# Cluster products with 32 moving columns, transform constants in six pieces, conversions at other steps, and a gated MLP without GpSimd's multiplication

## The chip, the core and the metric

The kernel runs on one core of a Trainium2 chip. The core has a matrix engine (PE, with PEld for its weight loads), three engines for elementwise work (DVE, ACT, POOL) and SP, whose queue issues most of the transfers (DMA); POOL issues a few as well. The metric is the time of one execution on the device, in microseconds (us), lower is better. Before the change it is 743.91 us (median of 3 runs, 739.0 to 745.26).

## What is computed

Three stages follow each other: attention in which a query sees only the keys of its own cluster, a Fourier mixing with a first MLP, and a second MLP with a convolution and a gate. All is float32; the matrix work is done with operands split into a high and a low part.

```python
# attention: B=2, H=8, S=768, D=64, 16 centroids per head
q_assign = argmax(einsum('bhsd,hcd->bhsc', q_n, c_n))   # and k_assign
mask   = q_assign[..., :, None] == k_assign[..., None, :]
scores = where(mask, scale * q @ k.T, -1e9)
attn   = softmax(scores) ; x = attn @ v                 # to [B, S, 512]
# mixing and first MLP (512 -> 2048 -> 512)
u  = x + real(fft(fft(x, axis=1), axis=2))
x  = u + relu(layernorm(u) @ w_ch1) @ w_ch2
# second MLP (512 -> 1024 -> 512)
h    = relu(x @ w_in)
gate = sigmoid(conv_w[0]*h[s-1] + conv_w[1]*h[s] + conv_w[2]*h[s+1])
out  = (h * gate) @ w_out
```

## The kernel before

**Attention in steps.** The 16 pairs of batch and head are cut into 6 tiles of 128 queries each, so there are 96 tiles, and one loop goes over steps n from -8 to 105. The order of all instructions in this part is the one written out by hand. In step n PE makes the scores of tile n+8 (`score_max`, L530 and L532) and DVE reduces them to the row maxima m (L535); PE makes the scores of tile n again, transposed (`score_exp`, L564 and L566), ACT takes their exponential (L572) and casts it to 16 bits (L584), POOL or, for tiles listed in `LO_ON_DVE`, DVE makes the low part (L592), and PE multiplies tile n-3 with the values (`attn_v`, L604). Three PSUM tiles of two banks take turns for all scores (`slot`), so PE can start a score only when the reduction or exponential of the third product back is done.

**Work that comes every 12 steps.** Two heads share one load, numbered m = 0 to 7. With k = 12m - 24, `load_raw` is issued at step k, `prep_sims` (the cluster products, L404, with a maximum L408 and a comparison L410 on DVE) at k+5, the high and low parts of q and k (`prep_hi`, `prep_lo`) at k+8 to k+11, `prep_turn` at k+11, `load_v` at k+14, `v_max` (a DVE reduction over the loaded values, L489) at k+16, and `v_turn` with four small DVE operations (`v_step`) at k+18. Four lists say where in a step something stands: `pre` before the scores, `mid` after PE's scores, `aft`, `post` and `fill` after the tile's own work. Every engine takes its instructions strictly in this order, so one that waits holds up all behind it.

**Cluster products.** `prep_sims` makes 12 products per pair of heads. Each loads 128 columns of q or k as weights and moves the centroid matrix W through, 128 columns of which only the first 32 are ever other than zero for this pair; a product's surplus columns are overwritten by the next.

**Conversions ahead.** The weights come as 64-bit words and are made into float32 by five operations (`from64`, L283 to L288; four on DVE and a square on ACT, L285). Four quarter loads of 512 columns are converted during attention: `ahead_start` issues the load three steps before the first operation, `ahead_store` writes the result to memory one step after the last. `AHEAD_STEPS` holds five steps for each of the four groups.

**Transform constants.** `DC` (two parts of 128 x 3342 float32) is loaded from POOL's queue at steps 20 and 32, `OD` at step 33; the first product that reads them is at step 60.

**Second MLP.** `mlp2_up` makes 128 of the 1024 hidden columns for 768 tokens: PE's product u, ACT's relu into h2 (L820), DVE's three convolution operations into cv (L822 to L824), ACT's sigmoid (L825), POOL's product with h2 (L826), and DVE's high and low part gH and gL (L828, L829). ACT casts the weights' high part (L792), POOL subtracts for the low part (L794). `down` multiplies gH and gL with w_out. PE's order is up 0, up 1, up 2, down 0, up 3, down 1 and so on, 16 of each over both batches; on the other engines the scheduler orders the work by its own rules.

Of the kernel before, what the change touches and what calls it, by code (L numbers as in the profile page):

```python
# [15 lines left out]
AF = mybir.ActivationFunctionType  # L16
ALU = mybir.AluOpType
# [2 lines left out]

B, H, S, D = 2, 8, 768, 64

DFT_LOADS = (20, 32)
LO_ON_DVE = {n for n in range(87) if n % 12 in (1, 2, 7, 11)} | {87}

AHEAD = 4
AHEAD_STEPS = [12 * q + n for q in range(4) for n in (17, 17, 18, 18, 22)]

IN_PLACE = range(89, 96, 2)
C = 16  # L30
# [9 lines left out]
C_CS, C_SS, C_CD, C_SD, C_END = 0, 1158, 2310, 2826, 3342  # L40
# [4 lines left out]
def tile_net(ctx, tc, qk, v, cen, w12, w34, conv, dft, odd, out):  # L45
    nc = tc.nc
    V, A, G, T = nc.vector, nc.scalar, nc.gpsimd, nc.tensor
# [264 lines left out]
    with ExitStack() as actx:  # L312
# [47 lines left out]
        t = slot("warm_up")  # L360
# [39 lines left out]
        def prep_sims(m):  # L400
            raw = raws[m]
            sm = sims[m] = first_bank("sim1") if m == 1 else slot(f"sim{m}")[:, 0]
            for t in range(12):
                T.matmul(sm[:, 32 * t:32 * t + 128], raw[:, t // 6, (t % 6) * 128:(t % 6) * 128 + 128],  # L404
                         W[:, m % 4, :], start=True, stop=True)
            sv = sm[:, 0:384].rearrange("p (g h c) -> p h g c", g=12, h=2)
            mx = ep.tile([128, 2, 12], F32, tag="mx", bufs=1, name=f"mx{m}")
            V.tensor_reduce(mx, sv, AX.X, ALU.max)  # L408
            eq = eqs[m] = ep.tile([128, 24, C], F16, tag="eq", bufs=1, name=f"eq{m}")
            V.tensor_tensor(eq.rearrange("p (h g) c -> p h g c", h=2), sv,  # L410
                            mx.unsqueeze(3).to_broadcast([128, 2, 12, C]), ALU.is_equal)
# [211 lines left out]
        def at(where, step, *f):  # L623
            where.setdefault(step, []).append(f)

        for m in range(1, NH // 2):
            k = 12 * m - 24
            if m > 1:
                at(pre, k, load_raw, m)
                at(post, k + 5, prep_sims, m)  # L630
                at(fill, k + 6, prep_first, m)
                at(fill, k + 7, prep_pick, m)
                at(fill, k + 8, prep_hi, m, (0,))
                at(fill, k + 9, prep_lo, m, 0, V)
                at(fill, k + 10, prep_hi, m, (1,))
                at(mid, k + 11, prep_turn, m)
                at(fill, k + 11, prep_lo, m, 1)
            at(fill, k + 14, load_v, m)
            at(fill, k + 16, v_max, m)
            at(mid, k + 18, v_turn, m)  # L640
            for i in range(4):
                at(aft, k + 18, v_step, m, i)
            at(fill, k + 22, v_step, m, 4)
            at(fill, k + 25, v_step, m, 5)
        at(fill, -8, prep_first, 1)
# [107 lines left out]
        for n in range(-LEAD, 6 * NH + 10):  # L753
# [11 lines left out]
            for f in aft.get(n, []) + post.get(n, []) + fill.get(n, []):  # L765
                f[0](*f[1:])
            if n in DFT_LOADS:
                i = DFT_LOADS.index(n)
                G.dma_start(out=DC[:, i], in_=dft[:, i])
            if n == DFT_LOADS[1] + 1:  # L770
                G.dma_start(out=OD, in_=odd)
            if n == 6 * NH - 10:
                ectx.close()
# [37 lines left out]
    def mlp2_up(b, f):  # L811
# [7 lines left out]
            up_half(o, w, xs[b], i)  # L819
            A.activation(h2[:, 1 + 384 * i:385 + 384 * i], o, AF.Relu)  # L820
        t = gp.tile([128, S], F32, tag="cv", bufs=2, name=f"cv{b}{f}")
        V.tensor_scalar(t, h2[:, 0:S], cw[:, 3 * f:3 * f + 1], None, ALU.mult)  # L822
        V.scalar_tensor_tensor(t, h2[:, 1:S + 1], cw[:, 3 * f + 1:3 * f + 2], t, ALU.mult, ALU.add)  # L823
        V.scalar_tensor_tensor(t, h2[:, 2:S + 2], cw[:, 3 * f + 2:3 * f + 3], t, ALU.mult, ALU.add)  # L824
        A.activation(t, t, AF.Sigmoid)  # L825
        G.tensor_mul(t, t, h2[:, 1:S + 1])  # L826
        g = hs[1, b, f] = [gp.tile([128, S], F32R, tag=n, bufs=2, name=f"{n}{b}{f}") for n in ("gH", "gL")]
        V.tensor_copy(g[0], t)  # L828
        V.tensor_sub(g[1], t, f32(g[0]))  # L829

    def down(s, g, f, side, when=(2,)):
# [163 lines left out]
```

## Time and profile before

| | |
|---|---|
| median of 3 runs | 743.91 us |
| profiled execution, its own time | 743.33 us |
| its span, first to last instruction | 741.5 us |
| PE busy | 694.9 us (94%) |
| DVE busy | 531.4 us (72%) |
| ACT busy | 346.8 us (47%) |
| POOL busy | 269.6 us (36%) |
| mean granted clock of PE | 0.984 of full |

Attention ends near 296 us, the first MLP near 589 us, the second at the end. A busy PE in this profile is one with a product in flight, not one at its peak. Idle times stand in square brackets behind an instruction, with what ended them.

### The profile page before, as it was taken

To read this page: it belongs to the slowest core of one execution; us is meant where nothing else is said; L and a number is where in the kernel's file an instruction comes from. 1 tells how busy PE (TensorE), PEld (TensorE's weight loads), DVE (VectorE), ACT (ScalarE), POOL (GpSimd) and SP (SyncE) were. 2 spreads that over 40 slices of the span, in tenths; PEclk is the share of its full clock that TensorE was granted. 3 is DMA by queue.
4 is the path that set the end of the run, shared out by engine and by line. 5 is a ranking of instruction groups with operands and counts; after the bars stand their busy time and mean duration, and the time that the engine had idled before them with its cause. 6 is when DMAs were issued, how large, how long until landed. Compare 5 with 4: busy or idle time off the path is not lost.

```text
span 741.5 us, 12519 instructions
## 1 busy us (share of the span) xinstructions
PE 694.9 (94%) x5090; PEld 618.4 (83%) x5090; DVE 531.4 (72%) x753; ACT 346.8 (47%) x493; POOL 269.6 (36%) x189
## 2 busy tenths in 40 slices
PE   8898999898898998989999999999999999999996
PEld 5697788787797886878988999999999888898984
DVE  7778989799977997999389938764111268777664
ACT  3476868586457687424234423443222233333321
POOL 8064544446244454121132012222332254444441
PEclk9999999999799999999999999999999999999999
DMA  7738678463532332324013421430000000002002
GB/s 213 183 71 213 183 198 248 121 179 79 151 78 58 89 107 95 114 77 179 29 44 127 156 72 61 166 114 1 1 0 1 1 0 1 1 1 85 1 1 85
DMA packets 19937, 66.47 MB, mean 90 GB/s; under 512 B 2868, under 2 KB 5928, under 8 KB 16808
## 3 DMA queue, kind: packets, MB, share of 16 engines
q1 hardware_dynamic: 19448, 61.93, 28.9%
q0 software_dynamic: 432, 3.75, 1.5%
q8 instruction: 40, 0.66, 0.4%
q14 instruction: 17, 0.14, 0.1%
HBM read 40.94 MB, written 5.77 MB: 63 GB/s over the span
## 4 chain that ended last, share of the span: by engine, by line
PE 45%; DVE 35%; DMA 5%; POOL 5%; ACT 4%; issue 3%; SPq 1%; POOLq 0%; DVEq 0%
DVE m L535 5%; PE acc L82 5%; DVE gH L828 5%; PE acc L80 5%; PE acc L81 5%; PE up L82 5%; PE up L80 5%; PE up L81 5%; DMA vraw<-v 4%; POOL cv L826 3%; PE av L604 3%; DVE cv L823 2%; DVE cv L824 2%; PE t L564 2%; PE s L530 2%
## 5 line engine op out<-in xcount | busy, mean ns | idle before, releaser
L592 POOL TENSOR_TENSOR p<-p,p 128x768 f16<-128x768 f32 x61 | 108.3, 1778 | 113.2 <-ACT p L584 83.0
L572 ACT ACTIVATE p<-t,cbias 128x768 f32<-128x768 f32 x92 | 82.7, 899 | 51.7 <-PE t L566 50.9
L535 DVE TENSOR_REDUCE m<-s 128x1 f32<-128x768 f32 x96 | 90.1, 943 | 11.7 <-PE s L532 6.6
L80 PE MATMUL up<-un,wha 128*128 128x384 f32 x248 | 84.2, 340 | 1.5 <-DVE firste L809 0.7
L82 PE MATMUL up<-un,wla 128*128 128x384 f32 x248 | 83.9, 339 | 1.6 <-DVE wla L794 1.6
L794 POOL TENSOR_TENSOR wla<-wa,wha 128x1024 fp32r<-128x1024 f32 x16 | 38.5, 2407 | 126.5 <-ACT wha L792 126.5
L81 PE MATMUL up<-un,wha 128*128 128x384 f32 x248 | 83.8, 338 | 0.0
L809 DVE SCALAR_TENSOR_TENSOR hL<-up,hH 128x384 fp32r<-128x384 f32 x62 | 34.2, 551 | 65.5 <-ACT hH L808 65.4
L604 PEld LDWEIGHTS <-p 128*128 128x128 f16 x1728 | 60.1, 99 | 18.0 <-issue 15.5
L584 ACT CAST p<-p 128x768 f16<-128x768 f32 x88 | 73.0, 830 | 1.4
L604 PE MATMUL av<-V,p 128*128 128x65 f16 x1728 | 71.7, 196 | 2.0 <-POOL p L592 2.0
L80 PE MATMUL acc<-wha,hH 128*128 128x512 f32 x186 | 73.6, 396 | 0.0
L82 PE MATMUL acc<-wha,hL 128*128 128x512 f32 x186 | 72.6, 391 | 0.0
L81 PE MATMUL acc<-wla,hH 128*128 128x512 f32 x186 | 72.5, 390 | 0.0
L564 PE MATMUL t<-X 128*128 128x384 f32 x192 | 55.6, 371 | 15.5 <-DVE m L535 14.1
L808 ACT ACTIVATE hH<-up 128x384 fp32r<-128x384 f32 x62 | 30.5, 491 | 75.7 <-PE up L82 75.6
L530 PE MATMUL s<-X 128*128 128x384 f32 x192 | 56.8, 377 | 5.9 <-DVE m L535 4.9
L828 DVE CAST gH<-cv 128x768 fp32r<-128x768 f32 x16 | 35.4, 2212 | 31.3 <-POOL cv L826 31.3
L792 ACT CAST wha<-wa 128x1024 fp32r<-128x1024 f32 x31 | 32.6, 1050 | 52.2 <-PE acc L82 46.2
L826 POOL TENSOR_TENSOR cv<-cv,h 128x768 f32<-128x768 f32 x16 | 25.5, 1591 | 78.0 <-ACT cv L825 78.0
L564 PEld LDWEIGHTS t<-X 128*128 128x128 f32 x192 | 31.8, 193 | 24.2 <-DVE m L535 15.2
L566 PE MATMUL t<-Y 98*128 98x384 f32 x192 | 50.9, 347 | 0.1
(314 smaller groups left out, 1644.3 us busy)
## 6 DMA issues: line engine op xcount, KB each, us to landing
rawa<-w SPq DMA_DIRECT2D x14, 1024.0 KB
rawb<-w SPq DMA_DIRECT2D x8, 1024.0 KB
raw<-qk SPq DMA_DIRECT2D x7, 768.0 KB
X<-G SPq DMA_DIRECT2D x14, 384.0 KB
Y<-G SPq DMA_DIRECT2D x14, 384.0 KB
DC<-dft POOLq DMA_DIRECT2D x2, 1671.0 KB, 7.0
vraw<-v SPq DMA_DIRECT2D x8, 384.0 KB
out<-y SPq DMA_DIRECT2D x12, 256.0 KB
```

The source lines that it names most:

```text
L80: T.matmul(o, sH, mH, start=start, stop=False)
L81: T.matmul(o, sH, mL, start=False, stop=False)
L82: T.matmul(o, sL, mH, start=False, stop=stop)
L530: T.matmul(t[:, c, 0:384], X[:, 0, sl], X[:, 1, 384 * c:384 * c + 384], start=True, stop=False)
L535: V.tensor_reduce(m6s[h][:, i:i + 1], t[:, :, 0:384], AX.XY, ALU.max, negate=True)
L564: T.matmul(t[:, c, 0:384], X[:, 1, sl], X[:, 0, 384 * c:384 * c + 384], start=True, stop=False)
L566: T.matmul(t[:, c, 0:384], Y[0:98, 1, sl], Y[0:98, 0, 384 * c:384 * c + 384], start=False, stop=True)
L572: A.activation(p, t[:, :, 0:384], AF.Exp, bias=cbias, scale=0.125)
L584: A.copy(p16[:, 0], p32s[n])
L592: eng.tensor_sub(p16[:, 1], p, p16[:, 0])
L604: T.matmul(o, p16[:, k, 128 * j:128 * j + 128], v16[:, i, h % 2, 65 * part:65 * part + 65], start=(i + j + k + part == 0), stop=(i == 5), ...
L828: V.tensor_copy(g[0], t)
```

## The change

The cluster products move 32 columns of W instead of 128. The constants DC are loaded in six pieces at steps 8, 20, 21, 32, 33 and 44, and OD at step 45. The first group of conversions stands at steps 10, 10, 11, 11, 13, and the other three where groups one to three stood before, so each group is a period of 12 steps earlier or nearly so and none is left in steps 53 to 58. `v_max` goes from k+16 to k+17, `v_turn` and the first four `v_step` from k+18 to k+19. In the second MLP the first convolution operation goes from DVE to ACT, the gate's product from POOL to DVE, and the cast to gH from DVE to ACT.

```diff
-DFT_LOADS = (20, 32)
+DFT_LOADS = (8, 20, 21, 32, 33, 44)
-AHEAD_STEPS = [12 * q + n for q in range(4) for n in (17, 17, 18, 18, 22)]
+AHEAD_STEPS = [10, 10, 11, 11, 13] + [12 * q + n for q in range(1, 4) for n in (5, 5, 6, 6, 10)]
...
             for t in range(12):
-                T.matmul(sm[:, 32 * t:32 * t + 128], raw[:, t // 6, (t % 6) * 128:(t % 6) * 128 + 128],
-                         W[:, m % 4, :], start=True, stop=True)
+                T.matmul(sm[:, 32 * t:32 * t + 32], raw[:, t // 6, (t % 6) * 128:(t % 6) * 128 + 128],
+                         W[:, m % 4, 0:32], start=True, stop=True)
...
-            at(fill, k + 16, v_max, m)
-            at(mid, k + 18, v_turn, m)
+            at(fill, k + 17, v_max, m)
+            at(mid, k + 19, v_turn, m)
             for i in range(4):
-                at(aft, k + 18, v_step, m, i)
+                at(aft, k + 19, v_step, m, i)
...
             if n in DFT_LOADS:
-                i = DFT_LOADS.index(n)
-                G.dma_start(out=DC[:, i], in_=dft[:, i])
-            if n == DFT_LOADS[1] + 1:
+                i, part = divmod(DFT_LOADS.index(n), 3)
+                part = slice(*((C_CS, C_SS), (C_SS, C_CD), (C_CD, C_END))[part])
+                G.dma_start(out=DC[:, i, part], in_=dft[:, i, part])
+            if n == DFT_LOADS[-1] + 1:
                 G.dma_start(out=OD, in_=odd)
...
-        V.tensor_scalar(t, h2[:, 0:S], cw[:, 3 * f:3 * f + 1], None, ALU.mult)
+        A.activation(t, h2[:, 0:S], AF.Copy, scale=cw[:, 3 * f:3 * f + 1])
...
-        G.tensor_mul(t, t, h2[:, 1:S + 1])
+        V.tensor_mul(t, t, h2[:, 1:S + 1])
...
-        V.tensor_copy(g[0], t)
+        A.copy(g[0], t)
```

On DVE around step 28 (m is the row maxima of two neighbouring tiles, vsc the maximum over the loaded values, U the attention's output, mx and eq the work on the cluster products), before:

```order
L535 TENSOR_REDUCE m_6_1427<-s_1428 128x1
L489 TENSOR_REDUCE vsc_1468<-vraw_1387 128x1
L617 SCALAR_TENSOR_TENSOR U<-av_1165,vsc_473,d_1389 128x6x64
L535 TENSOR_REDUCE m_6_1427<-s_1471 128x1
L283 TENSOR_SCALAR ahead<-ahead 128x512
L284 SCALAR_TENSOR_TENSOR ahead<-ahead 128x512
L408 TENSOR_REDUCE mx_1520<-sim_1507 128x24
L410 TENSOR_TENSOR eq_1522<-sim_1507,mx_1520 128x384
L535 TENSOR_REDUCE m_6_1427<-s_1529 128x1
```

The same place after the change:

```order
L535 TENSOR_REDUCE m_6_1436<-s_1437 128x1
L617 SCALAR_TENSOR_TENSOR U<-av_1173,vsc_525,d_1398 128x6x64
L535 TENSOR_REDUCE m_6_1436<-s_1478 128x1
L283 TENSOR_SCALAR ahead<-ahead 128x512
L284 SCALAR_TENSOR_TENSOR ahead<-ahead 128x512
L408 TENSOR_REDUCE mx_1527<-sim_1514 128x24
L410 TENSOR_TENSOR eq_1529<-sim_1514,mx_1527 128x384
L489 TENSOR_REDUCE vsc_1531<-vraw_1396 128x1
L535 TENSOR_REDUCE m_6_1436<-s_1538 128x1
```

The reduction over the values (L489) has moved behind one row maximum, two conversions and the work on the cluster products.

On DVE around step 11, in the first period of 12 steps (G is the low part of k in `prep_lo`), before:

```order
L535 TENSOR_REDUCE m_3_688<-s_689 128x1
L617 SCALAR_TENSOR_TENSOR U<-av_413,vsc_175,d_649 128x6x64
L535 TENSOR_REDUCE m_3_688<-s_732 128x1
L461 TENSOR_TENSOR G_647<-raw_337,G_647 128x768
L535 TENSOR_REDUCE m_3_688<-s_783 128x1
```

The same place after the change:

```order
L535 TENSOR_REDUCE m_3_691<-s_692 128x1
L283 TENSOR_SCALAR ahead<-ahead 128x512
L284 SCALAR_TENSOR_TENSOR ahead<-ahead 128x512
L617 SCALAR_TENSOR_TENSOR U<-av_413,vsc_175,d_651 128x6x64
L535 TENSOR_REDUCE m_3_691<-s_737 128x1
L286 SCALAR_TENSOR_TENSOR ahead<-ahead 128x512
L461 TENSOR_TENSOR G_649<-raw_337,G_649 128x768
L535 TENSOR_REDUCE m_3_691<-s_790 128x1
```

Three conversion operations have come in, one of them (L286, behind ACT's square) directly ahead of `prep_lo`.

On ACT in the second MLP, one hidden block in the second batch (h is the relu, cv the convolution and sigmoid, whb the weights' high part), before:

```order
L820 ACTIVATE h_7438<-u_7441 128x384
L820 ACTIVATE h_7438<-u_7455 128x384
L825 ACTIVATE cv_7469<-cv_7469 128x768
L792 CAST whb_5_7560<-wb_6212 128x1024
L820 ACTIVATE h_7501<-u_7504 128x384
```

The same block after the change:

```order
L821 ACTIVATE h_7442<-u_7445 128x384
L821 ACTIVATE h_7442<-u_7459 128x384
L823 ACTIVATE cv_7473<-h_7442,cw 128x768
L826 ACTIVATE cv_7473<-cv_7473 128x768
L793 CAST whb_5_7564<-wb_6216 128x1024
L829 CAST gH_7479<-cv_7473 128x768
L821 ACTIVATE h_7505<-u_7508 128x384
```

ACT has two more operations in a block, the first convolution operation ahead of the sigmoid and the cast to gH behind the weight cast; on PE only the width of the cluster products and the step of `v_turn` differ, beside two products of the first `down` that change places.

## Rows read from the trace of the kernel before

**Rows 1.** Page, part 1: busy us (share of the span) xinstructions, first engines.
```profile
PE 694.9 (94%) x5090; PEld 618.4 (83%) x5090; DVE 531.4 (72%) x753; ACT 346.8 (47%) x493; POOL 269.6 (36%) x189
```
**Rows 2.** Waits of the whole run: who waited for whom, us, times, longest.
```profile
DVE vsc L489 <- DMA vraw<-v: 13.0, 4, 4.8
```
**Rows 3.** Timeline 127 to 143 us: start, us, engine, what, [idle before].
```profile
132.45 2.92 PE L404 MATMUL sim<-W,raw 128*128 128x128 f32 x24
...
135.57 0.95 DVE L489 TENSOR_REDUCE vsc<-vraw 128x1 f32<-128x768 f32 x1 [4.83 <-DMA vraw<-v]
...
137.96 1.01 PE L530 MATMUL s<-X 128*128 128x384 f32 x2 [2.59 <-DVE m L535]
```
**Rows 4.** Stretches: us, busy PE, PEld, DVE, ACT, POOL, granted clock, DMA share, GB/s.
```profile
138.00:141.00 3.00, 3.00 (x10) 2.81 (x10) 2.89 (x6) 0.00 (x0) 0.89 (x1) 0.50 0.42 88
186.00:196.00 10.00, 8.04 (x53) 6.95 (x54) 9.92 (x12) 3.56 (x5) 3.52 (x3) 0.50 0.43 114
```
**Rows 5.** Tile "ahead", its DVE operations: ns min/median/max, first and last start us.
```profile
L283 DVE TENSOR_SCALAR ahead<-ahead x4: 415/417/417, 73.1 to 170.3; 128x512 int32<-128x512 int32 x4
L284 DVE SCALAR_TENSOR_TENSOR ahead<-ahead x4: 692/693/694, 73.5 to 170.7; 128x512 int32<-128x512 int32 x4
...
L286 DVE SCALAR_TENSOR_TENSOR ahead<-ahead x4: 672/673/2105, 76.8 to 174.0; 128x512 uint32<-128x512 uint32 x4
L288 DVE SCALAR_TENSOR_TENSOR ahead<-ahead x4: 682/842/1005, 84.4 to 189.9; 128x512 f32<-128x512 f32 x4
```
**Rows 6.** Timeline of PE, 176 to 190 us: two products that had waited.
```profile
177.06 0.62 PE L564 MATMUL t<-X 128*128 128x384 f32 x2 [1.09 <-DVE m L535]
...
186.82 0.98 PE L564 MATMUL t<-X 128*128 128x384 f32 x2 [2.99 <-DVE m L535]
```
**Rows 7.** Timeline 54 to 61 us, DVE and PE in steps 11 and 12.
```profile
55.60 0.96 DVE L535 TENSOR_REDUCE m<-s 128x1 f32<-128x768 f32 x1 [1.95 <-ACT ohT L431]
56.47 2.41 DVE L461 TENSOR_TENSOR G<-raw,G 128x768 fp32r<-128x768 f32 x1
...
59.80 0.62 PE L564 MATMUL t<-X 128*128 128x384 f32 x2 [0.86 <-DVE m L535]
```
**Rows 8.** Timeline of PEld, 43 to 46 us: weight loads of 16-bit and 32-bit tiles.
```profile
43.70 0.61 PEld L604 LDWEIGHTS <-p 128*128 128x128 f16 x18 [0.16 <-issue]
44.25 0.30 PEld L530 LDWEIGHTS s<-X 128*128 128x128 f32 x2
```
**Rows 9.** Instructions by line and form: cluster products' loads, and constants' issues on POOL.
```profile
L404 PEld LDWEIGHTS sim<-W,raw 128*128 128x128 f32 x168 | 19.3, 192 | 0.6 <-ACT W L383 0.6
L769 POOL DMA_DIRECT2D DC<-dft x2 | 1.3, 673 | 0.0
```
**Rows 10.** Waits of PE, 580 to 742 us: us, times, longest.
```profile
PE acc L80 <- DVE gH L828: 1.6, 1, 1.6
PE acc L82 <- DVE gL L829: 1.4, 2, 1.1
PE acc L80 <- DVE y L847: 1.1, 1, 1.1
PE u L80 <- DVE x L868: 1.0, 1, 1.0
```
**Rows 11.** One DVE round of the second MLP as a stretch, columns as in Rows 4.
```profile
699.80:708.87 9.07, 9.07 (x47) 8.11 (x46) 6.32 (x7) 2.56 (x4) 3.94 (x2) 1.00 0.00 0
```
**Rows 12.** Timeline of PE: the first product of two neighbouring up blocks.
```profile
700.38 0.34 PE L80 MATMUL u<-x,whb 128*128 128x384 f32 x1
...
708.82 0.34 PE L80 MATMUL u<-x,whb 128*128 128x384 f32 x1
```
**Rows 13.** By line and form: count, busy us, mean ns, idle before; elementwise work of one tile.
```profile
L824 DVE SCALAR_TENSOR_TENSOR cv<-h,cw,cv 128x768 f32<-128x768 f32 x16 | 16.3, 1017 | 0.5
L829 DVE TENSOR_TENSOR gL<-cv,gH 128x768 fp32r<-128x768 f32 x16 | 15.3, 957 | 1.3
L510 ACT ACTIVATE V<-vraw,vsc 128x768 f16<-128x768 f32 x8 | 7.4, 922 | 0.7 <-DVE vsc L508 0.7
```

## The prediction

> **What bounds the kernel now.** I read the page's busy times first. PE has a product in flight for 694.9 of 741.5 us [rows 1], so little can be won that is not PE's own time or a stretch in which PE stands still. By stage, the timeline shows two kinds of loss in attention, which is the first 296 us. One is a DVE that waits: four of the eight reductions over the loaded values (L489) stand still for their transfer, 13.0 us in all, the longest 4.8 us [rows 2], and DVE takes its work in order, so the row maxima behind them are late. The other is a DVE with too much to do in one place, around 177 to 192 us. In both cases PE runs out of free score tiles: it has three, and the third product back must have been reduced. What PE then loses it loses twice, since its granted clock falls to half of 2.4 GHz: 0.50 in 138 to 141 us and through 186 to 196 us [rows 4], each after a standstill of 2.6 to 3 us [rows 3, 6]. In the second MLP PE comes to a new up block every 8.44 us [rows 12], while one DVE round takes 9.07 us [rows 11]; PE is ahead by two blocks, so it stands still only at the start, where the batches change, and at the end [rows 10].
>
> **v_max one step later.** Take the longest wait. The reduction stands from 130.7 to 135.6 us, and the products for the clusters run on PE from 132.45 to 135.4 [rows 3]. Then PE stands for 2.59 us, because the next row maximum (0.95 us) and what follows it are behind the reduction. After the change DVE first makes that row maximum, two conversions (0.42 and 0.69 us [rows 5]) and the cluster work, and comes to the reduction only behind PE's last cluster product at 135.4 us, when the values have landed or nearly so. The scores are then released before PE is done with the cluster products. The row maximum behind the reduction comes one reduction (0.95 us) later than it could, most of it beside PE's next scores; I leave 0.3 us for it, so 2.3 of 2.59 us go. With no such standstill the clock should not fall: the 3 us at half speed [rows 4] hold 1.5 us of work at full speed. Term: **-3.8 us**. Below it is nothing, if the conversions now ahead of the reduction wait for their own load, which is queued just in front of the values; above it is -6, if the smaller standstills behind the other three waits go as well. I take the case counted out here. The four small operations of v_step and the turn go a step later and have until step k+22; that slack is the cover, and without it the values would be scaled one step late, 2.7 us a load if 296 us are spread over some 110 steps.
>
> **Conversions.** No group is left in steps 53 to 58. There the last group took 0.42, 0.69, 2.10 and 0.68 us of DVE [rows 5] (of L286 the longest, which is its last, and of L288 the shortest, as it began at 189.9), 3.9 us together, 3.2 of them before PE's long wait at 186.8. PE stood for 1.09 and 2.99 us there [rows 6], and DVE was busy for 9.92 of the 10 us from 186 to 196 [rows 4], so its work sets the pace and what is taken from it comes back. Of 3.9 us I count 3.3, because DVE then meets PE's own pace sooner. Below is nothing. Above is -9: both standstills (4.1 us) and half of the ten slow microseconds (5). I stay near the lower end because the mixing's folds in the same steps keep DVE full.
>
> The first group now stands in steps 10 to 13. Its first two operations, 1.1 us, fall into the 1.95 us in which DVE waits for ACT [rows 7], so they cost nothing; without that wait they would cost their 1.1. The third needs ACT's square of the same step and stands ahead of prep_lo. By the rows, prep_lo began at 56.47 and the next row maximum only after its 2.41 us, and PE had already stood 0.86 us [rows 7]. The third operation adds its 0.67 us [rows 5] and about 1.2 us of waiting for the square, less what prep_lo regains if POOL is no longer at work beside it. Term: **+1.5 us**, between +0.5 and +4 (2.4 us of waiting and work, and a fallen clock at 1.5). The store of this group now stands ahead of the next load and of the values on SP's queue and waits for the conversion in step 13. Behind it are the load of the second group and the values of m = 2; these have the step that v_max was given, about 2.5 us, as cover, and if it is gone the first wait of rows 2 stays as it was. Conversions: **-1.8 us** together.
>
> **Cluster products with 32 columns.** Each float32 product is two instructions, 24 for a pair of heads: 168 loads for seven pairs [rows 9], 2.92 us to the end of the last [rows 3], so one comes every 0.115 us. With a quarter of the columns the moving part would shrink, but every instruction also loads 128 columns of 32-bit weights. The trace shows how fast such loads can follow each other where nothing holds them: two of them take 0.30 us [rows 8], one alone takes 0.19 [rows 9], so the second starts 0.11 us after the first. The weight load then sets the pace: 24 x 0.11 = 2.64 instead of 2.76 us, and the last product ends some 0.08 us sooner. That is 0.2 us a pair, eight pairs: **-1.5 us**, and nothing where DVE is behind anyway. The other bound is the 16-bit tiles, where 18 loads take 0.61 us [rows 8], 0.03 us each: 24 x 0.033 = 0.8, or 2 us less a pair, 16 in all. I stay with the nearest row, since it is the same form of load.
>
> **Constants in six pieces.** The bytes are the same. Four more issues at 0.67 us of POOL [rows 9] make 2.7 us on an engine that is idle for most of the span [rows 1], so I count nothing; where POOL had a low part waiting, each would delay it by 0.67. All pieces are issued by step 45, fifteen steps ahead of their first use.
>
> **Gated MLP.** PE's standstills for gH and gL are 1.6 and 1.4 us, of which 1.9 stand at the end, where DVE's slower rounds have used up PE's lead; those for x and y are 1.0 and 1.1 [rows 10]. The new round: ACT's work in one DVE round is 2.56 us [rows 11], and it gains the first convolution operation (0.92 us, by a scaled pass of the same size) and the cast to gH (0.83 to 0.92), so some 4.3 us. Between them DVE has two multiply-adds of 1.02 us; its new product of 0.96 us lies beside the weight cast on ACT [rows 13]. That makes 6.4 us with a little for the hand-overs, less than PE's 8.44, so PE's lead holds to the end. Of 3.0 us for gH and gL I count 2.7, of x all of 1.0, of y half: **-4.2 us**. If a DVE operation with two inputs is drawn out by POOL's subtraction as prep_lo was (2.41 us [rows 7] against 0.96 [rows 13]), the round grows to 7.9 us and still fits. Bounds: -2 (two such stretches, 9.3 us, and the end as now) and -5.1, all four waits.
>
> **The sum.** -3.8 - 1.8 - 1.5 - 4.2 = -11.3 us against 743.3 us of the profiled execution (span 741.5 and 1.8 around it), which is 0.6 us under the median: **732.0 us**.
>
> **Rivals.**
> *The loads do not bind (faster).* If 32 columns bring the products to the pace of the 16-bit tiles, 14.4 us more go, less what DVE holds back in its full stretches: 717.6 at the best and about 720. For it speaks that loads and products overlap well; against it the 0.30 us of rows 8. The Trainium skill, page "TensorE: Matmul & The Clock Gate", section "Back-to-back issue gap", gives a start-to-start floor of about 25 ns for 1 to 64 columns; by it a pair would take 0.6 us. [...]
> *The clock falls (slower).* A cluster product now moves a quarter of the columns in about the same 2.6 us. If the granted clock drops behind each of the seven products in the loop, and stays down for 10 us as at 186 us [rows 4], each costs 5 us: 732 + 35 = 767. If it stays down for 3 us as at 138, each costs 1.5: 742.5, no change. It decides from 2.8 us a product (19.3 us to the bound of slower, over seven). Against it: there was no standstill in these places, and PE's other work stands close on both sides.
> *The waits come back.* The conversions now ahead of v_max wait for their load, SP is held by the store, and the last steps of attention's heavy period stay full for the folds: the first two terms become +1.5 in place of -5.6 and the rest stays: 739. For it speaks that this load is queued just in front of the values.
>
> **Chances.** My forecast 0.56 (its own range 725 to 737), the loads that do not bind 0.13, the fallen clock 0.15 (0.07 of it slower, 0.08 no change), the waits that come back 0.16. About 1%, 7.4 us, is what a measurement of this kernel can tell from no change. Faster: 0.56 less 0.02 at its edge, 0.13, and 0.05 of the last: 0.72. No change: 0.02, 0.08 and 0.11: 0.21. Slower: 0.07. The range that holds 8 in 10 reaches from 718, inside the first rival, to 741, inside the last two.
>
> **What would show it.** Right: waits of L489 for vraw under 3 us in all; no half clock at 138 and less than 5 us of it near 186; PE's standstill in step 12 up to 2 or 3 us; cluster products at 2.6 to 2.8 us; no wait for gH or gL at the end, and DVE rounds of 8.4 us in the second MLP. Wrong: cluster products near 1 us, a granted clock of 0.50 behind them, conversions that wait for their load in step 17, or ACT as what PE waits for in the second MLP.

## The result and the profile after

The changed kernel takes 734.35 us (median of 4 runs, 733.92 to 736.4) beside 743.42 for the kernel before: a ratio of 0.9895, with a 95% interval of 0.986 to 0.993 (the quotient of the two medians is 0.988; the range below goes by the ratios). Six more runs of it later gave 734.59 us and 0.9875 (0.984 to 0.991). So it is faster, by 7.8 to 9.3 us where 11.3 were forecast: 734.35 against 732.0, inside the range. Two terms of the sum were wrong by more than that 2.4 us, in opposite directions.

The page of the changed kernel, part 1, which answers to [rows 1]:

```profile
PE 696.4 (95%) x5090; PEld 623.2 (85%) x5090; DVE 526.9 (72%) x737; ACT 376.2 (51%) x525; POOL 245.2 (33%) x177
```

PE is busy for 1.5 us longer although the span is 9.3 us shorter (732.2 against 741.5), and although its cluster products move only a quarter of the columns. Products that move less and take longer point to a lower clock.

To see where time is won and lost, I compare the start of the same instruction in both traces. The exponentials of ACT (one for each tile) serve in attention; later it is PE's first up product and its last product.

| place in the program | before, us | after, us | difference | change since the row above |
|---|---|---|---|---|
| exponential of tile 0 | 29.50 | 31.49 | +1.99 | +1.99 |
| tile 6 | 43.96 | 45.73 | +1.77 | -0.22 |
| tile 15 | 65.00 | 69.49 | +4.49 | +2.72 |
| tile 39 | 127.85 | 132.12 | +4.27 | -0.22 |
| tile 42 | 141.42 | 141.34 | -0.08 | -4.35 |
| tile 51 | 162.44 | 163.31 | +0.87 | +0.95 |
| tile 60 | 193.78 | 192.07 | -1.71 | -2.58 |
| first up product, second MLP | 589.01 | 587.33 | -1.68 | +0.03 |
| end of PE's last product | 736.70 | 727.37 | -9.33 | -7.65 |

Attention, forecast at -7.1 us, gives 1.7. The second MLP, forecast at -4.2, gives 7.65. Four rows of the table carry the story.

**Ahead of the loop: +2.0 us, with the clock at half.** Stretches of the changed kernel (us, busy PE, PEld, DVE, ACT, POOL, granted clock, DMA share, GB/s): the one ahead of the loop, one behind the cluster products of the pair m = 3, and the two of [rows 4]:

```profile
9.40:19.60 10.20, 10.20 (x50) 9.01 (x50) 5.43 (x13) 2.82 (x5) 6.72 (x6) 0.50 0.68 153
77.60:81.00 3.40, 3.40 (x27) 3.09 (x26) 3.37 (x6) 2.00 (x3) 0.91 (x1) 0.50 0.99 192
137.00:141.00 4.00, 4.00 (x34) 3.92 (x32) 3.97 (x3) 1.26 (x2) 2.84 (x2) 1.00 0.88 182
186.00:196.00 10.00, 8.25 (x63) 7.27 (x62) 8.93 (x11) 4.12 (x6) 2.74 (x3) 0.66 0.59 132
```

Before the change, the stretch from 9.40 to 19.60 ran at 1.00, and the second set of cluster products in it took 2.94 us:

```profile
9.40:19.60 10.20, 9.00 (x65) 7.59 (x66) 7.86 (x16) 3.83 (x6) 6.72 (x6) 1.00 0.80 184
```

```profile
9.72 2.94 PE L404 MATMUL sim<-W,early 128*128 128x128 f32 x24 [0.42 <-DMA early<-qk]
```

The timeline of PE in the changed kernel at the start of the first two stretches (start, us, engine, what):

```profile
9.17 5.00 PE L404 MATMUL sim<-W,early 128*128 128x32 f32 x24
14.10 1.45 PE L441 MATMUL fm<-ident,oh 128*16 128x128 f16 x12
...
73.48 0.73 PE L604 MATMUL av<-V,p 128*128 128x65 f16 x18
74.05 2.84 PE L404 MATMUL sim<-W,raw 128*128 128x32 f32 x24
76.73 0.60 PE L530 MATMUL s<-X 128*128 128x384 f32 x2
77.16 0.52 PE L532 MATMUL s<-Y 96*128 96x384 f32 x2
77.52 0.74 PE L564 MATMUL t<-X 128*128 128x384 f32 x2
78.06 0.84 PE L566 MATMUL t<-Y 98*128 98x384 f32 x2
```

None of these rows has an idle time in brackets. From 9.4 us on the clock is at half, right after the second set of cluster products has begun at 9.17, and the set takes 5.00 us; at 77.6 it falls 0.7 us behind such a set. PE had not stood still just ahead of either place. The falls of [rows 4] came with standstills of 2.6 to 3 us.

The 1.99 us of the table are not the price of this fall alone. The start of the first exponential lies anywhere from 27.60 to 30.99 us in the eleven traces, of the kernel before and of the experiments below, that have 64 or 128 columns here and the full clock. A closer measure is from the start of the second set to the first scores (L530): 8.11 us in the changed kernel against 5.98 before, so the fall costs 2.1 us up to there. (It is 7.6 in the two other traces with 32 columns here, and 5.8 to 6.0 in nine of the eleven. In the other two, e4 and e10, it is 7.3 and 7.1, since PE there waits 1.6 and 1.4 us for DVE.)

**Behind the long wait: -4.35 us.** L489 no longer waits for vraw anywhere, and at 138 the clock is full. The changed kernel's timeline there:

```profile
136.54 1.65 POOL L592 TENSOR_TENSOR p<-p,p 128x768 f16<-128x768 f32 x1
136.71 1.77 DVE L283 TENSOR_SCALAR ahead<-ahead 128x512 int32<-128x512 int32 x1
136.90 2.84 PE L404 MATMUL sim<-W,raw 128*128 128x32 f32 x24
138.37 1.65 POOL L592 TENSOR_TENSOR p<-p,p 128x768 f16<-128x768 f32 x1 [0.18 <-ACT p L584]
138.51 2.06 DVE L284 SCALAR_TENSOR_TENSOR ahead<-ahead 128x512 int32<-128x512 int32 x1
139.58 0.59 PE L530 MATMUL s<-X 128*128 128x384 f32 x2
140.49 0.55 DVE L408 TENSOR_REDUCE mx<-sim 128x24 f32<-128x384 f32 x1
141.54 0.94 DVE L489 TENSOR_REDUCE vsc<-vraw 128x1 f32<-128x768 f32 x1
```

PE goes from its cluster products straight into scores (no bracket at 139.58, where [rows 3] had 2.59 us). But the two conversions that now lie in DVE's former wait take 1.77 and 2.06 us, not 0.42 and 0.69 [rows 5]. Experiment e12 below shows why: POOL's subtractions (L592) run beside them.

**Steps 10 to 15: +2.7 us,** of which 0.8 belong to `v_max` (e4 below). DVE, POOL and PE of the changed kernel where the first group of conversions now stands, to be read against [rows 7]:

```profile
56.02 2.03 DVE L284 SCALAR_TENSOR_TENSOR ahead<-ahead 128x512 int32<-128x512 int32 x1
...
58.93 1.66 POOL L592 TENSOR_TENSOR p<-p,p 128x768 f16<-128x768 f32 x1 [1.43 <-ACT p L584]
...
59.37 1.77 DVE L286 SCALAR_TENSOR_TENSOR ahead<-ahead 128x512 uint32<-128x512 uint32 x1
61.06 0.95 DVE L461 TENSOR_TENSOR G<-raw,G 128x768 fp32r<-128x768 f32 x1
...
62.93 0.61 PE L564 MATMUL t<-X 128*128 128x384 f32 x2 [1.09 <-DVE m L535]
```

The third conversion no longer waits for ACT's square, as I had counted, since L284 ahead of it takes 2.03 us; it is itself drawn out by 1.1 us. PE stands at 59.50, 62.93 and 66.04, 2.8 us in all.

**Second MLP: -7.65 us.** What PE waits for in the changed kernel from 580 us to the end is one row, and [rows 10] are gone:

```profile
PE u L82 <- POOL wlb L795: 1.6, 1, 1.6
```

This row stands at the head of the stage in both kernels. One DVE round of the changed kernel as a stretch, against 9.07 us in [rows 11], and then, from its timeline, POOL's subtraction in that round with the gate's low part beside it:

```profile
690.98:699.42 8.44, 8.44 (x44) 7.62 (x43) 5.43 (x6) 4.55 (x6) 2.43 (x1) 1.00 0.00 0
```

```profile
694.95 2.43 POOL L795 TENSOR_TENSOR wlb<-wb,whb 128x1024 fp32r<-128x1024 f32 x1 [6.00 <-ACT whb L793]
...
695.83 2.37 DVE L830 TENSOR_TENSOR gL<-cv,gH 128x768 fp32r<-128x768 f32 x1 [0.77 <-ACT gH L829]
```

The stretch is as long as PE's own pace, 8.44 us, even with gL drawn out from 0.96 [rows 13] to 2.37 us.

### The profile page after: what moved, and what is told of

It is laid out like the page before. It is cut to its first block, busy times and chain, and to the rows that moved or that the text cites. A ratio compares the mean times of both kernels' runs of the same rounds, so it can differ in the third digit from the quotient of the medians.

```text
span 732.2 us, 12502 instructions
## 1 busy us (share of the span) xinstructions
PE 696.4 (95%) x5090; PEld 623.2 (85%) x5090; DVE 526.9 (72%) x737; ACT 376.2 (51%) x525; POOL 245.2 (33%) x177
## 4 chain that ended last, share of the span: by engine, by line
PE 65%; DVE 26%; issue 3%; POOL 2%; ACT 2%; DMA 1%; SPq 0%; DVEq 0%; POOLq 0%; ACTq 0%
PE acc L80 8%; PE acc L81 8%; PE acc L82 8%; DVE m L535 6%; PE up L82 5%; PE up L80 5%; PE up L81 5%; PE av L604 3%; PE u L82 3%; PE u L80 3%; PE u L81 3%; PE sim L404 2%; PE s L530 2%; PE t L564 2%; PE s L532 2%
## 5 line engine op out<-in xcount | busy, mean ns | idle before, releaser
L592 POOL TENSOR_TENSOR p<-p,p 128x768 f16<-128x768 f32 x61 | 106.5, 1748 | 117.9 <-ACT p L584 79.6
L795 POOL TENSOR_TENSOR wlb<-wb,whb 128x1024 fp32r<-128x1024 f32 x16 | 39.0, 2446 | 96.4 <-ACT whb L793 79.4
L530 PE MATMUL s<-X 128*128 128x384 f32 x192 | 58.5, 387 | 1.1 <-DVE m L535 0.8
L532 PE MATMUL s<-Y 96*128 96x384 f32 x192 | 51.2, 349 | 0.0
```

The costliest lines, as they stand in the source:

```text
L530: T.matmul(t[:, c, 0:384], X[:, 0, sl], X[:, 1, 384 * c:384 * c + 384], start=True, stop=False)
L532: T.matmul(t[:, c, 0:384], Y[0:96, 0, sl], Y[0:96, 1, 384 * c:384 * c + 384], start=False, stop=True)
L592: eng.tensor_sub(p16[:, 1], p, p16[:, 0])
L795: eng.tensor_sub(wl, w32[k, f], f32(wh))
```

## Experiments

All ratios are to the kernel before, measured on the same chip, with 95% intervals.

### e1 and e2: only the width of the cluster products

e1 is the changed kernel with wide products, e2 the kernel before with narrow ones.

```diff
-                T.matmul(sm[:, 32 * t:32 * t + 32], raw[...], W[:, m % 4, 0:32], ...)   # e1
+                T.matmul(sm[:, 32 * t:32 * t + 128], raw[...], W[:, m % 4, :], ...)
```

> The changed kernel with only the cluster products put back to 128 moving columns. Theory A (the narrow products let the granted clock fall: in the changed kernel it stands at 0.50 from 9.35 to 19.6 us, where before it was full, and from 77.6 to 81.0 right behind the products of one pair): both half-clock stretches go, the 1.99 us by which the first exponential is late go to under 0.3, each product takes 2.92 us again, and the time falls by 2 to 4 us, to about 731 us (ratio to before 0.983 to 0.987). Theory B (the half clock there has another cause, and the narrow products only save 0.08 us each): the half clock stays, and the time is 734 to 736 us.

> The kernel before with only the cluster products cut to 32 moving columns. Theory A (the clock falls behind narrow products): the granted clock stands at 0.50 before the first step for some 10 us, the first exponential comes 2 us later, and the time rises by 2 to 4 us, to 745 to 748 us (ratio 1.002 to 1.006). Theory B (no effect on the clock): 743 us or up to 1.5 us less, as the sum of the prediction had it.

**Measured:** e1 731.81 us, 0.9826 (0.980 to 0.985), the full clock from 9.4 to 19.6, and the first exponential 0.5 us earlier than before the change. e2 747.71 us, 1.0052 (1.003 to 1.008). PE of e1 ahead of the loop, then three stretches of e2 at half clock, ahead of the loop and close behind the products of two pairs (its cluster products run from 40.95 to 43.79 and from 104.82 to 107.66; behind the second of these PE also stood 0.88 us). The trace of e2 is that of its slowest execution, 751.79 us:

```profile
9.04 2.84 PE L404 MATMUL sim<-W,early 128*128 128x128 f32 x24
```

```profile
10.20:16.90 6.70, 6.70 (x37) 5.69 (x37) 4.48 (x11) 1.75 (x3) 6.11 (x5) 0.50 0.80 176
44.40:47.60 3.20, 3.20 (x26) 2.89 (x26) 2.79 (x8) 1.07 (x2) 0.92 (x1) 0.50 1.03 208
109.20:112.40 3.20, 3.20 (x27) 2.89 (x26) 3.06 (x9) 0.88 (x2) 0.92 (x1) 0.50 0.79 164
```

**What follows:** the width alone makes the kernel before slower, by 0.5% or 4 us, and taking it back makes the changed kernel faster by 2.5 to 5 us. It does so through the clock. The mean granted clock of an execution was 0.968 to 0.979 in e2's twelve executions (0.987 in the middle of 23 executions of the kernel before, none below 0.982; in later ones a single 0.980), 0.978 to 0.985 in the ten of the changed kernel, and 0.990 to 0.992 in the five of e1. Theory A holds in place and sign; which stretches fall, and for how long, differs from trace to trace. In the four traces with 32 columns in the loop (the changed kernel, e2, e5 and e9) the clock falls within 1.5 us of the end of 7 of 24 sets; in the ten traces with 64 or 128 columns there, within 2.5 us of the end of none of 60.

### e5 and e6: which products, and how wide

e5 keeps 128 columns for m = 0 and 1 and 32 for the others; e6 moves 64 in all.

```diff
+                c = 128 if m < 2 else 32        # e5; e6: c = 64
-                T.matmul(sm[:, 32 * t:32 * t + 32], raw[...], W[:, m % 4, 0:32], ...)
+                T.matmul(sm[:, 32 * t:32 * t + c], raw[...], W[:, m % 4, 0:c], ...)
```

> The changed kernel with 128 moving columns for the two pairs of heads whose cluster products stand ahead of the loop (m = 0 and 1), and 32 for the six in the loop. With all eight wide the ratio was 0.9826, with all eight narrow 0.9895, so the width is worth 0.7% or 5 us. If the fall of the clock ahead of the loop (10.2 us at 0.50 in the changed kernel) is all of it: 0.983, 731 us. If the products in the loop carry their share (half clock behind some of them, as at 77.6 us): about 0.986, 733 us, and the half clock ahead of the loop is gone while one or two stretches of 3.4 us behind a narrow product stay.

> The changed kernel with 64 moving columns in all cluster products. If the weight loads set the pace, 24 instructions take 2.84 us again, as with 32. If what the clock answers to is how much PE moves, 64 columns lie between: half clock for fewer microseconds than with 32 (27 us before 296 us of the span) and more than with 128 (10), ratio 0.985 to 0.988. If the clock depends on something else than the width, e.g. on where PE comes in time, 64 is like 128 or like 32: 0.983 or 0.9895.

**Measured:** e5 732.48 us, 0.9861 (0.983 to 0.989); e6 731.66 us, 0.9842 (0.981 to 0.987). Weight loads and products by form (ns min/median/max, first and last start), two rows of the changed kernel in the loop and two ahead of it:

```profile
L404 PEld LDWEIGHTS sim<-W,raw x168: 186/192/192, 6.2 to 213.0; 128*128 128x128 f32 x168
L404 PE MATMUL sim<-W,raw x168: 273/276/297, 6.2 to 213.1; 128*128 128x32 f32 x168
L404 PEld LDWEIGHTS sim<-W,early x24: 190/333/338, 9.1 to 13.7; 128*128 128x128 f32 x24
L404 PE MATMUL sim<-W,early x24: 195/401/402, 9.2 to 13.8; 128*128 128x32 f32 x24
```

The same of e6 ahead of the loop, and two stretches of e5:

```profile
L404 PEld LDWEIGHTS sim<-W,early x24: 190/192/192, 9.2 to 11.7; 128*128 128x128 f32 x24
L404 PE MATMUL sim<-W,early x24: 222/275/275, 9.3 to 11.8; 128*128 128x64 f32 x24
```

```profile
104.60:108.10 3.50, 3.50 (x27) 3.19 (x26) 3.46 (x6) 1.11 (x2) 1.03 (x2) 0.51 0.97 207
210.50:213.90 3.40, 3.40 (x27) 3.10 (x26) 2.14 (x3) 0.90 (x1) 0.92 (x1) 0.51 0.92 189
```

**What follows:** with wide products ahead of the loop the half clock from 9.4 us on is gone, and in the loop two stretches behind narrow products stay (e5's products end at 104.45 and 209.73), as expected. With 64 columns no product is followed by half clock: in this kernel, 64 is like 128. The intervals of e1, e5 and e6 overlap, so how the cost divides between the two places is not settled. The weight load takes 192 ns at full clock whatever the width and 333 ns at half clock, and the set of 24 takes 2.84 us with 32 columns, 2.87 with 64 and 2.92 with 128: the loads set the pace, and the narrow products save 0.08 us a set, where the sum had counted 0.2.

### e3: the gated MLP alone

The kernel before with the three operations of the gated MLP on the engines of the change.

```diff
-        V.tensor_scalar(t, h2[:, 0:S], cw[:, 3 * f:3 * f + 1], None, ALU.mult)
+        A.activation(t, h2[:, 0:S], AF.Copy, scale=cw[:, 3 * f:3 * f + 1])
-        G.tensor_mul(t, t, h2[:, 1:S + 1])
+        V.tensor_mul(t, t, h2[:, 1:S + 1])
-        V.tensor_copy(g[0], t)
+        A.copy(g[0], t)
```

> The kernel before with only the gated MLP's three operations on other engines. By the prediction's term: -4.2 us, between -2 and -5.1, 739 us (ratio 0.994). By the comparison of the two profiles, in which the lag of the changed kernel goes from -1.7 at step 93 to -9.3 at the end: -7.6 us, 736 us (ratio 0.990). If part of the 7.6 came with the changed order in attention, it lies between; the waits of PE for gH, gL, x and y are gone in any case.

**Measured:** 735.46 us, 0.9877 (0.985 to 0.990), that is -7 to -11 us. In its trace the second MLP is 7.6 us shorter, as in the changed kernel and in e1.

**What follows:** this term is the largest, and all of it belongs to this edit. Behind the wait of 1.6 us at the head of the stage, which stays, PE's listed standstills go from 6.15 us in seven places to 0.13: 6.0 us. The other 1.6 is what a standstill costs beside its own length. A standstill of the kernel before, in PE's timeline:

```profile
604.62 0.40 PE L81 MATMUL acc<-wlb,gH 128*128 128x512 f32 x1
606.08 0.50 PE L82 MATMUL acc<-whb,gL 128*128 128x512 f32 x1 [1.06 <-DVE gL L829]
606.41 0.39 PE L80 MATMUL acc<-whb,gH 128*128 128x512 f32 x1
606.64 0.40 PE L81 MATMUL acc<-wlb,gH 128*128 128x512 f32 x1
```

From 604.62 to 606.41 two products take 1.79 us, where two at their usual pace of 0.23 take 0.46: 1.33 us lost, of which the bracket shows 1.06. The bracket counts from the modelled end of the product ahead, 0.40 us after its start, while at the usual pace the next one starts after 0.23; and the product behind the wait is followed after 0.33 us, not 0.23. In the seven places the same sum gives 0.23 to 0.27 us beside the bracket, 1.8 us together, near the 1.6.

### e4: v_max one step later, alone

```diff
-            at(fill, k + 16, v_max, m)
+            at(fill, k + 17, v_max, m)
-            at(mid, k + 18, v_turn, m)
+            at(mid, k + 19, v_turn, m)
-                at(aft, k + 18, v_step, m, i)
+                at(aft, k + 19, v_step, m, i)
```

> The kernel before with only v_max, v_turn and the first four v_step one step later. By the prediction's term: -3.8 us (739.5 us, ratio 0.995): no wait of L489 for vraw of more than 3 us in all, no standstill of 2.6 us at 138 and no half clock behind it. By the rival that the conversions, now ahead of the reduction, wait for their own load: waits of L283 of over 2 us, and 742 to 744 us. The conversions still stand in steps 17 to 22 of each period here, so the half clock from 186 to 196 stays in both.

**Measured:** 741.64 us, 0.9963 (0.994 to 0.999), -1.1 to -4.4 us. L489 has no wait left, and the stretch around 138 runs at full clock. L283 waits for its load 1.1 us in three places. Between tiles 6 and 9 the kernel loses 0.8 us. The stretch, and one conversion by form (ns min/median/max):

```profile
138.00:142.00 4.00, 3.62 (x44) 2.91 (x43) 3.97 (x6) 2.28 (x4) 1.92 (x2) 1.00 0.79 158
```

```profile
L284 DVE SCALAR_TENSOR_TENSOR ahead<-ahead x4: 2043/2051/2068, 73.9 to 167.0; 128x512 int32<-128x512 int32 x4
```

**What follows:** the mechanism is the forecast one, and the size is -2.75 us by the ratio, with -3.8 still inside the interval. Two costs were missing. In the first period of the loop (m = 1) the reduction used to lie in a gap in which DVE waits for the cluster products; a step later it stands behind them and makes a row maximum late (the 0.8 us). And the conversions, no longer behind a waiting reduction, run beside POOL's subtraction: L284 takes 2.05 us in the middle where it took 0.69 (e12). What that costs the kernel was not measured by itself.

### e7 and e8: the conversions

Both are e1 with other steps for the conversions: e7 those of before, e8 another place for the first group.

```diff
-AHEAD_STEPS = [10, 10, 11, 11, 13] + [12 * q + n for q in range(1, 4) for n in (5, 5, 6, 6, 10)]
+AHEAD_STEPS = [12 * q + n for q in range(4) for n in (17, 17, 18, 18, 22)]                        # e7
+AHEAD_STEPS = [12, 12, 13, 13, 15] + [12 * q + n for q in range(1, 4) for n in (5, 5, 6, 6, 10)]  # e8
```

> The changed kernel with 128 moving columns and with the conversions at their steps of before, 17 to 22 of each period. Against all eight products wide (0.9826) this is the term of the conversions, forecast at -1.8 us, in the place where the change has it. By the forecast the time is 1.8 us more (0.985): the first group no longer costs (the first exponentials of steps 10 to 15 come 2 us sooner), steps 53 to 58 have their group again and lose 3 us, with half clock from 186 to 196. If the first group costs as much as the last one gained (2.6 us each in the comparison of the profiles), the time is the same, 0.982 to 0.983.

> The changed kernel with 128 moving columns and the first group of conversions at steps 12, 12, 13, 13, 15 instead of 10, 10, 11, 11, 13, so that its last operations no longer stand ahead of prep_lo in step 11, and SP meets its store later. If the 2 us that steps 10 to 15 lose come from the operations ahead of prep_lo, 1 to 2 us come back: 0.980 to 0.981, 730 us. If DVE has no room anywhere in this period, nothing changes: 0.9826, 731.8 us.

**Measured:** e7 732.78 us, 0.9863 (0.983 to 0.990); e8 731.93 us, 0.9850 (0.982 to 0.988); e1, for both, 731.81 and 0.9826. By the start of exponentials, from tile 6 to 15 e7 loses 0.8 us (which is v_max's) where e1 loses 2.8, and from tile 54 to 60 it gains nothing (+0.6) where e1 gains 1.9.

**What follows:** the first group costs 2.0 us in its new place, of which 1.2 come back by tile 18 in e1, and the last group's leaving brings 2.5 by tile 60. Both are differences of two traces, and the second varies. From tile 54 to 90, against the kernel before, the other traces with 128 columns and the old steps lie at -1.1 (e3), +0.7 (e4) and +1.8 us (e7), those with the new steps at -1.5 (e1 and e8) and -3.0 (e10): some 2.3 us apart in the mean, with a spread as large. Part of it is the clock: around 186 us half clock lasts 10.2 us in the kernel before and in e7, but 3.4 in e3 with the same steps, as in e1, e8 and e10. The net is a gain of 0.6 us by the two profiles, 1.0 by the medians and 2.7 by the ratios (e1 ran on another chip), and the intervals of the ratios overlap, so nothing at all is not excluded. e8 moves the loss, not its size: it is as late at tile 15 (+2.55 us against e1's +2.06). Neither place that was tried in that period is free.

### e9 and e10: the changed kernel again, and the constants

e10 is e1 with DC in two pieces.

```diff
-DFT_LOADS = (8, 20, 21, 32, 33, 44)
+DFT_LOADS = (20, 32)
```

> The changed kernel once more, beside the two below on one chip, since its ratio (0.9895, interval 0.986 to 0.993) rests on four executions. If the width of the cluster products costs 5 us (0.9895 against 0.9826 with all wide, and +3.9 us when they alone are narrowed), the ratio is again 0.988 to 0.991, 735 us. If the first four executions were by chance late, it is 0.985 or less, like the kernels with 64 and 128 columns.

> The changed kernel with 128 moving columns and the constants DC in two pieces at steps 20 and 32 again. The forecast counted the six pieces as nothing: the ratio is then that of all eight products wide, 0.982 to 0.985. If four more issues on POOL or other transfers beside the values' cost or bring more than 1 us, it leaves this band: below 0.981 the pieces cost, above 0.986 they help.

**Measured:** e9 734.59 us, 0.9875 (0.984 to 0.991); e10 731.96 us, 0.9845 (0.981 to 0.988), on one chip.

**What follows:** every one of the ten executions of the changed kernel lies at 732.5 us or above, every one of e1's five at 732.5 or below. e9's trace has the half clock ahead of the loop again (10.2 to 17.0 us), and in the loop behind two other narrow products, at 44.4 and 170.6 and not at 77.6. The pieces of DC do nothing that can be measured.

### e11: room for DVE

e6 with v_max, v_turn and v_step of m = 1 at their old steps, and a part of the mixing's fold one step earlier.

```diff
+            at(fill, k + 17 - (m == 1), v_max, m)      # so too v_turn and v_step
-        plan = (("even0", fill, 54), ...
+        plan = (("even0", fill, 53), ...
```

> The changed kernel with 64 moving columns, and two steps moved: v_max, v_turn and v_step of m = 1 go back to where they were (in the first period the reduction filled a gap of DVE, and behind the cluster work it makes the row maximum of step 6 late, which all kernels with the later step show as 0.8 us between steps 6 and 9), and the first part of the mixing's fold (L108 to L110) goes from step 54 to 53, into room that the conversions have left, since PE stands for 2.8 us at step 56 behind it and prep_lo. If both readings are right, 0.8 us and 1 to 3 us come on top of the 64 columns: 0.980 to 0.982, 729 us. If DVE's work only moves the standstill elsewhere, 0.984, 731.5 us.

**Measured:** 730.94 us, 0.9826 (0.979 to 0.986). The 0.8 us between tiles 6 and 9 are gone (-0.07 there). PE's two late standstills are 1.34 and 2.76 us, where they were 2.84 and 0.69 in e6.

**What follows:** the reading of the first period holds. Around step 56 DVE's work only moves the standstill. It has the lowest median of the kernels that compute everything, 730.94, but the intervals of e1, e6, e10 and e11 overlap, so which is best is open. All four have lower medians (730.9 to 732.0) than the kernel before and the changed one, and e1's interval lies below the changed kernel's first one.

### e12: what draws the conversions out

e1, in which POOL writes zeros in place of the exponentials' low part for 16 tiles.

```diff
+            elif 12 <= n < 60 and n % 12 in (3, 4, 5, 6):
+                G.memset(p16[:, 1], 0.0)
             else:
                 eng.tensor_sub(p16[:, 1], p, p16[:, 0])
```

> The changed kernel with 128 moving columns, in which POOL does not compute the low part of the exponentials for 16 tiles (those with n from 12 to 59 and n mod 12 of 3 to 6) but writes zeros in its place; PE multiplies the zeros as before. These subtractions lie beside the conversions of steps 17 to 22, of which L284 takes 2.03 us in four of the kernels so far, where before the change it took 0.69. If DVE's conversions are drawn out by POOL's subtraction beside them, L284 takes 0.69 us and L283 0.42 in the three later groups, DVE is earlier, and 0 to 3 us come off the 731.8 us with wide products. If something else draws them out (the transfers that land then, for one), they keep their 2 us.

**Measured:** 727.33 us, 0.9784 (0.973 to 0.984). That is 4.5 us below e1 by the medians and 3.1 by the ratios, more than the 0 to 3 expected; what else the missing subtractions bring was not separated. The conversions by form (ns min/median/max), e12, then the changed kernel, then L284 in e1:

```profile
L283 DVE TENSOR_SCALAR ahead<-ahead x4: 427/428/429, 53.1 to 133.0; 128x512 int32<-128x512 int32 x4
L284 DVE SCALAR_TENSOR_TENSOR ahead<-ahead x4: 693/694/2031, 53.6 to 133.5; 128x512 int32<-128x512 int32 x4
```

```profile
L283 DVE TENSOR_SCALAR ahead<-ahead x4: 427/1126/1770, 55.6 to 136.7; 128x512 int32<-128x512 int32 x4
L284 DVE SCALAR_TENSOR_TENSOR ahead<-ahead x4: 2014/2040/2058, 56.0 to 138.5; 128x512 int32<-128x512 int32 x4
```

```profile
L284 DVE SCALAR_TENSOR_TENSOR ahead<-ahead x4: 693/2025/2045, 53.6 to 136.5; 128x512 int32<-128x512 int32 x4
```

**What follows:** without POOL's subtractions beside them the three later groups take 0.43 and 0.69 us; the first group, whose subtractions stay, keeps its 2.03 us. In the rows around 138 us, POOL's subtraction ends at 140.02 and L284 at 140.57, 0.55 us later and not much less than the operation takes alone: DVE's operation stood until POOL's was done. In all four groups of the changed kernel L284 ends 0.54 or 0.55 us behind a subtraction that began before it. And in e1, which computes everything, the one L284 that found POOL idle (at 136.46) took 0.69 us. L283, which reads one tensor, is drawn out too, from 0.42 to 1.77 us at 136.71. The Trainium skill, page "SBUF — State Buffer", section "SBUF: two separate sides", states this as a lock: a port pair goes to whichever of the two starts first, for the whole instruction, and a DVE operation with two inputs in that memory meets it against a GpSimd operation that reads there. The trace agrees, with 2.03 us beside a subtraction against 0.69 without one. POOL's zeros fell beside none of the L284, so no run here shows what an operation that only writes would do.

## Why the prediction was right or wrong

**v_max (-3.8, measured -2.75 alone, between -1.1 and -4.4).** Right in its mechanism: no wait of L489, no standstill and no half clock at 138. The step that the trace contradicts is "most of it beside PE's next scores; I leave 0.3 us for it". It held for the place that I worked out and not for the first period, which I did not look at and where the wait had cost nothing: 0.8 us were lost there. The term also took the conversions ahead of the reduction at 0.42 and 0.69 us; they take up to 1.77 and 2.06. The case that the conversions wait for their own load came only in part, 1.5 us in two places of the changed kernel and 2.9 in two of e1.

**Conversions (-1.8, measured -0.6 by the profiles, -1.0 by the medians and -2.7 by the ratios, and nothing at all is not excluded).** The last group's leaving brought some 2.3 to 2.5 of the 3.3 us, with a spread as large between traces. Little of it came back as less standing of PE: its standstills from 177 to 193 us are 4.6 us in the changed kernel where they were 5.2 (the two of [rows 6] and 1.14 at 192.03). The sign of less than 5 us of half clock near 186 was not met: they are 6.8, and 3.4 in e1. The first group lost 2.0, within its range but for another reason than the one given: not a wait for the square but L284 and L286 drawn out, 1.3 and 1.1 us. I had used "drawn out" for prep_lo and for the MLP and priced the moved conversions by rows in which they ran beside nothing. The 0.42, 0.69 and 0.67 us of [rows 5] were such ones: in the kernel before, DVE stood in its wait for the values while POOL subtracted.

**Cluster products (-1.5, measured +2.5 to +5).** The first half of the step was right in kind: the weight loads bind, and a set takes 2.84 us where 2.92 were, 0.08 less and not 0.2. The rival that the loads do not bind is gone. The start-to-start floor of 25 ns that the Trainium skill gives (page "TensorE: Matmul & The Clock Gate", section "Back-to-back issue gap") is not reached here: the 24 instructions of a set start 0.11 us apart. The second half, that nothing else changes, is the step that failed: the clock fell, and the term came out with the other sign. The rival of the falling clock was right in kind and wrong in two ways. I let it act behind each of seven products in the loop (there are six), with one price for all; in the changed kernel's profile it acted behind one of them, and in the second of the two sets ahead of the loop, which I had not looked at for this. And what spoke against it, that there was no standstill and that PE's other work stands close, did not keep the clock up. The Trainium skill, page "TensorE: Matmul & The Clock Gate", section "HAM oscillation — how this bites in real kernels", tells of the clock falling back in PE's waits for data. Here it fell with no wait in front of it (5.00 us for a set whose row has no bracket). Why it falls behind some narrow products and not behind others, I did not settle.

**Constants (0).** Right within what e10 can tell.

**Gated MLP (-4.2, measured -7.6 in the trace, 7 to 11 by the ratio).** Right in its mechanism: the DVE round now follows PE's pace, gL drawn out to 2.37 us still fits, and no wait is left at the end. The term was too small in two places. I counted 4.2 us of the four waits of [rows 10], but all of PE's waits behind the head of the stage went, 6.0 us, also those for h that I had not listed. And a standstill costs PE 0.23 to 0.27 us beside its listed length, 1.6 us in all. My bound of -5.1 was no bound, since it was the sum of the listed waits.

**The sum.** The width term came out 4 to 6.5 us worse and the MLP term 3.4 better than forecast; the other two lie within about 1 us of theirs. 732.0 was close because the two large misses nearly cancel. That was luck, and not a sign that each term was right. The rival in which the waits come back did not happen.

## What to carry to other kernels

Making a product cheaper for PE can cost more than it saves: where weight loads set the pace, fewer moving columns save next to nothing (0.08 us a set here), and the granted clock should be looked at behind them, also ahead of the loop. Price a moved DVE operation by what POOL does beside it in its new place, not by its duration in the old one. And count a standstill of PE with the start behind it, about 0.25 us more than the listed idle time here.

## What the runs showed of the hardware

- The granted clock fell to 0.50 while PE had a product in flight all the time: 10.20 of 10.20 us busy from 9.4 us on, with 24 products of 32 columns in 5.00 us. With 64 or 128 columns in the same place it stayed at 1.00, and the set took 2.79 and 2.84 us. Why some sets of 32 columns are followed by a fall and others are not stays open.
- At half clock the weight loads slow down too, from 192 to 333 ns, and so a set that is bound by its loads pays as well.
- A DVE operation (L284) that meets a POOL subtraction already running stands until that is done: 2.03 us instead of 0.69, and its end lies 0.54 or 0.55 us behind the end of the subtraction.
- A standstill of PE in the second MLP cost 0.23 to 0.27 us more than its listed length, in each of seven places.
